# A recurrent-attention and wave-mixing kernel: r loaded by whole batches, w spread by a matmul, and tasks that may choose their engine

## The chip, the core and the metric

The kernel runs on one core of one Trainium2 chip. The metric is the device time of one execution in microseconds. Before the change the median of three runs is 149.64 us (148.95 to 150.03).

The engines are named as in the profile: PE multiplies matrices and writes to PSUM (eight banks here), DVE, ACT and POOL work on vectors, SP issues most DMAs. Only PE, DVE and ACT reach PSUM.

## What is computed

Inputs r, k, v have the shape (4 batches, 8 heads, 768 tokens, 48), w and u (8, 48). Cut to what matters:

```
state = 0
for t in range(768):                       # for every batch and head
    cur = outer(u * k[t], v[t])
    y[t] = r[t] @ (state + cur)
    state = w[:, None] * state + outer(k[t], v[t])
x = y, heads side by side                   # (4, 768, 384)

theta = x @ w_theta
zr, zi = x * cos(theta), x * sin(theta)
mixed = w_tok_r @ zr + w_tok_i @ zi         # over the 768 tokens of a batch
un = x + mixed
out = un + relu(un @ w_ch)
```

## The kernel before

**Chunks.** A batch has six chunks of 128 tokens, treated in three pairs. Within a chunk the recurrence becomes matmuls: r is multiplied by a power of w that grows with the token's place in its chunk (`wpow`), k by the inverse power (`wpinv`). Then scores k·r, masked to earlier tokens, take the place of the recurrence inside a chunk, and a state per chunk (`Y`, `Z`, and `Sb` in bf16) carries what came before.

**One pair of chunks (`front`, from L421).** Tokens lie on the 128 partitions.

- Load r, k and v of two chunks (`load_tokens`, L352): two DMAs each of 192 KB, one per chunk. A run of 48 floats, 192 bytes, lies together in DRAM for each head and token.
- L436 multiplies r by `wpow` into `Rw` (on POOL, one of the first pair on DVE); L448 multiplies k by `wpinv` into `Kw` (DVE); L456 casts v (ACT).
- `flip6` (L410) transposes eight blocks of `Rw` on PE (L414), and ACT evacuates them into `RT` (L417); the same for `Kw` into `KT`.
- Scores (L470, PE), masked products into `mAT` (L475, DVE); the diagonal with u: PD = RT·KT (L481, DVE), a small matmul (L489), its copy (L494, ACT), and `yd` (L496, POOL).
- Outer products for the state (L509, PE), `Y` (L521 and L523, DVE), `Z` (L526, POOL), `Sb` (L529, ACT).
- y from the carried state (L544) and the scores (L558), added into x (L564, DVE).
- x is transposed (`flip6` again), theta (L581, PE), its sine and cosine (L585, L588, ACT), then zr (L591, DVE) and zi (L594, POOL).

**Token weights (L391 to L405).** Twelve loads of 384 KB, rows of w_tok_r and w_tok_i, are transposed in fp32 on PE (L393) and evacuated, one half on ACT (L404), the other on DVE (L402).

**Mixing (`mixing`, from L599).** For each of six output chunks of a batch, three tasks of four matmuls (L613), the residual (L621, DVE), a transpose, the channel matmul (L629), and relu and residual (L634, DVE), and a store (L637).

**Setup (`setup`, from L274).** L275 loads w, repeated for all 128 partitions, into `w_f` (192 KB); ACT takes its logarithm (L328) and two exponentials (L332 `wpow`, L335 `wpinv`). u and w are also loaded in a small tile `wu` through ACT's queue (L283, L284) and transposed on PE (L315). Two loads of ACT's function tables stand at L326 and L340.

**The order.** No engine's order is written by hand. Every step is a task of a `Plan`: an engine, a planned cost in ns, what it reads and writes, the PSUM banks that it takes, and a due number (`prio`, smaller first). `order` (L83) plays the tasks through in planned time: each engine takes, of the tasks that are ready, the one with the lowest due number. PE is charged 95 ns for a change of tile form. POOL's tasks and DVE's marked ones exclude each other. `search` (L153) shifts random due numbers 2000 times and keeps a shift if the planned end does not grow. The instructions are then issued in that order. Loads have due numbers far below the rest and so keep the order in which the program creates them; 12 buffers (`Ls`) serve as a ring for all loads of r, k, v and weights. SP takes the loads in order, and a load waits there until its buffer has been read.

Of the kernel before, what the change touches and what calls it, by code (L numbers as in the profile page):

```python
# [17 lines left out]
BF16 = mybir.dt.bfloat16  # L18
Alu = mybir.AluOpType
Act = mybir.ActivationFunctionType  # L20

ROUNDS = 2000
# [8 lines left out]
PE, DVE, ACT, POOL, SP = "PE", "DVE", "ACT", "POOL", "SP"  # L31


KEEP = 0
SWITCH = 95.0
STAY = 10.0
LATENCY = {PE: 200.0, DVE: 150.0, ACT: 175.0, POOL: 160.0, SP: 2200.0}


class Task:  # L40
    __slots__ = ("eng", "ns", "fn", "deps", "prio", "seq", "lat", "acq", "uses", "nwait",
                 "users", "ready", "end", "mode", "keep", "port")


class Plan:

# [8 lines left out]
    def add(self, eng, ns, fn, rd=(), wr=(), prio=0.0, lat=None, acq=(), use=(), mode=0, keep=0, port=False):  # L55
        t = Task()
        t.eng, t.ns, t.fn, t.prio, t.mode = eng, ns, fn, prio, mode
        t.keep, t.port = keep, port or eng == POOL
        t.lat = LATENCY[eng] if lat is None else lat
# [19 lines left out]
        t.deps = deps  # L79
        self.tasks.append(t)  # L80
        return t

    def order(self):  # L83
        for t in self.tasks:
            t.users, t.nwait, t.ready = [], len(t.deps), 0.0
        for t in self.tasks:
            for d in t.deps:
                d.users.append(t)
        waiting = {e: [] for e in (PE, DVE, ACT, POOL, SP)}
        for t in self.tasks:  # L90
            if t.nwait == 0:
                waiting[t.eng].append(t)
        free_at = {e: 0.0 for e in waiting}
# [6 lines left out]
        while len(out) < n:  # L100
            for e in waiting:
                while free_at[e] <= now:
                    nfree = sum(1 for b in banks if b[0] <= now)
                    best = None
                    for t in waiting[e]:
                        if t.port and e in (DVE, POOL) and held[POOL if e == DVE else DVE] > now:
                            continue
                        if t.ready <= now and (
                                not t.acq or len(t.acq) + t.keep <= nfree):
                            rank = (t.prio - (STAY if e == PE and t.mode == last_mode and last_mode else 0.0), t.seq)  # L110
                            if best is None or rank < top:
                                best, top = t, rank
                    if best is None:
                        break
                    t = best
                    waiting[e].remove(t)
                    banks.sort()
                    for b in t.acq:
                        self.bank_of[b] = banks.pop(0)[1]
                    ns = t.ns  # L120
# [4 lines left out]
                    free_at[e] = now + ns  # L125
                    if t.port:
                        held[e] = now + ns
                    done = now + ns
                    t.end = done + t.lat
# [6 lines left out]
                    for x in t.users:  # L136
                        x.ready = max(x.ready, done if x.eng == e else t.end)
                        x.nwait -= 1
                        if x.nwait == 0:
                            waiting[x.eng].append(x)  # L140
            nxt = [f for f in free_at.values() if f > now]
            nxt += [t.ready for e in waiting for t in waiting[e] if t.ready > now]
# [10 lines left out]
    def search(self, rounds, seed=0):  # L153

        rnd = random.Random(seed)
        pool = [t for t in self.tasks if t.eng != SP]
        best = self.span()
        for _ in range(rounds):
            some = rnd.sample(pool, rnd.choice((1, 3, 10, 40)))
            old = [t.prio for t in some]  # L160
            scale = rnd.choice((2, 6, 20))
            for t in some:
                t.prio += rnd.gauss(0, scale)
            got = self.span()
            if got <= best:
                best = got
            else:
                for t, p in zip(some, old):
                    t.prio = p
        return best  # L170


def rows_of(w, n):
    return dataclasses.replace(w, ap=[[0, n]] + [list(x) for x in w.ap])


def wide(ap, n):
    return dataclasses.replace(ap, ap=[list(x) for x in ap.ap] + [[0, n]])
# [3 lines left out]
def kernel(  # L182
# [27 lines left out]
    bank_t = [ps.tile([C, 512], F32, name=f"bank{i}") for i in range(8)]  # L210

# [12 lines left out]
    mask01 = sb.tile([C, C], BF16, name="mask01")  # L224
    pi2 = sb.tile([C, 1], F32, name="pi2")
    wu = sb.tile([2 * HP, 2, Dp], F32, name="wu")
    w_f = sb.tile([C, H, D], F32, name="w_f")
    lw_f = sb.tile([C, H, D], F32, name="lw_f")
    lw_p = sb.tile([C, HP], F32, name="lw_p")
    tok_f = sb.tile([C, 2], F32, name="tok_f")  # L230
    wpow = sb.tile([C, H, D], F32, name="wpow")
# [5 lines left out]
    NL = 12  # L237
    Ls = ring(NL, [C, 2 * HD], F32, "ld")
    Rws = ring(2, [C, 2, H, Dp], BF16, "Rw")
    Kws = ring(4, [C, 2, H, Dp], BF16, "Kw")  # L240
    vbs = ring(5, [C, 2, H, D], BF16, "vb")
    RTs = ring(4, [C, 2, HP, C], BF16, "RT")
# [21 lines left out]
    def act_ns(n, psum=True):  # L264
        return n / 1.2 + (60 if psum else 95)

    def dve_ns(n, rate=1.0):
        return n / (0.96 * rate) + 75

    def pool_ns(n):  # L270
        return 190 + 1.95 * n


    def setup():  # L274
        P.add(SP, 300, lambda: nc.sync.dma_start(out=w_f, in_=rows_of(w, C)),  # L275
              wr=["w_f"], prio=-2e6, lat=3000)

        def wu_fill():
            nc.vector.memset(wu, 0.5)
        P.add(DVE, 100, wu_fill, wr=["wu"], prio=-100)  # L280

        def wu_load():
            nc.scalar.dma_start(out=wu[:HP, :, :D], in_=w.rearrange("(a b) d -> a b d", b=2))  # L283
            nc.scalar.dma_start(out=wu[HP:, :, :D], in_=u.rearrange("(a b) d -> a b d", b=2))  # L284
        P.add(ACT, 200, wu_load, wr=["wu"], prio=-99, lat=3000)

        def tok():
            nc.gpsimd.iota(tok_f[:, 0:1], pattern=[[0, 1]], base=0, channel_multiplier=1,
                           allow_small_or_imprecise_dtypes=True)
        P.add(POOL, 200, tok, wr=["tok_i"], prio=-100)  # L290

        def tok2():
            nc.vector.tensor_scalar(tok_f[:, 1:2], tok_f[:, 0:1], -1.0, -1.0,
                                    op0=Alu.mult, op1=Alu.add)
            nc.vector.memset(pi2, math.pi / 2.0)
            nc.vector.memset(uw, 0.0)
        P.add(DVE, 300, tok2, rd=["tok_i"], wr=["tok_f", "uw", "pi2"], prio=-99)
# [4 lines left out]
        P.add(POOL, 500, lambda: make_identity(nc, ident_f), wr=["ident_f"], prio=-98)  # L302
        P.add(POOL, 500, lambda: make_identity(nc, ident), wr=["ident"], prio=-98)
        P.add(POOL, 600, lambda: pads(Rws), wr=[(("Rw", i), j) for i in range(2) for j in range(2)], prio=-97)
        P.add(POOL, 800, lambda: pads(Kws), wr=[("Kw", i) for i in range(4)], prio=-96)

        def mask():
# [4 lines left out]
        P.add(POOL, 1000, mask, wr=["mask"], prio=-95)  # L312

        def wu_flip():
# [3 lines left out]
        P.add(PE, 300, wu_flip, rd=["wu", "ident_f"], acq=["wu"], prio=-90)  # L318
        P.add(DVE, 100, lambda: nc.vector.tensor_copy(wup, bank("wu")[:, :2 * HP]),
              use=["wu"], wr=["wup"], prio=-90)  # L320
        def uw_fill():
            for hi in range(2):
                q = slice(hi * Dp, (hi + 1) * Dp)
                nc.vector.tensor_mul(uw[q, :, hi], wup[q, HP:], wup[q, :HP])
        P.add(DVE, 200, uw_fill, rd=["wup"], wr=["uw"], prio=-90)
        P.add(ACT, 1300, lambda: nc.scalar.preload_act_table_set("natural_log_exp_and_others"),  # L326
              wr=["act_ln"], prio=-98.5)
# [357 lines left out]
```

## Time and profile before

| | |
|---|---|
| median of three runs | 149.64 us |
| profiled execution | 148.95 us |
| its span, first to last instruction | 147.2 us |
| outside the span | 1.75 us |
| PE busy | 130.2 us, 89% |
| DVE, ACT, POOL busy | 114.8, 92.0, 79.4 us |
| DMA packets | 81084, of these under 512 bytes 75561 |
| DMA queue of SP | 24.98 MB, 69.9% of 16 engines' span |
| first r half landed, second | 5.23, 6.08 us |
| last token weights landed | about 37.1 us |
| first score matmul, first mixing matmul | 11.41, 40.50 us |

"Busy" is the union of the times of an engine's instructions. A PE matmul's time includes its way through the array, and the next one starts before it ends; the rate is read from start to start. A wait is put down to what was released last. "x" with a number counts instructions.

### The profile page before, as it was taken

Reading aid. Unit: us, or ns where it says so; the run is one execution under the profiler, and the core shown is the slowest. Engines: PE = TensorE matmul, PEld = TensorE weight load, DVE = VectorE, ACT = ScalarE, POOL = GpSimd, SP = SyncE. Lnnn points to the kernel's source line nnn. Section 1 sums busy time; section 2 is a strip of 40 time slices with the busy share of each in tenths; the row PEclk is TensorE's granted clock in tenths of the full one; section 3 lists DMA queues with packets and bytes.
Section 4 is the critical chain, followed back from the end, with each engine's and each line's share of the span. In section 5 each row is a group of like instructions: output and inputs, shape, how many; then the busy total and the mean of one; then the engine's idle time right before and its main releaser. Section 6 shows DMA issues by size and latency. Waiting matters only on the chain.

```text
span 147.2 us, 4185 instructions
## 1 busy us (share of the span) xinstructions
PE 130.2 (89%) x1641; PEld 91.3 (62%) x1641; DVE 114.8 (78%) x220; ACT 92.0 (63%) x175; POOL 79.4 (54%) x96
## 2 busy tenths in 40 slices
PE   0157687999999999999989999999999999999990
PEld 0036574879966776667746666677666666656640
DVE  0349869699954989999979999999899998442561
ACT  3484667878949368689473984899735467702140
POOL 7317937473735649868469779691552747400000
PEclk9999999999999999999999999999999999999999
DMA  2999988999999799899998997995000111120224
GB/s 71 225 216 223 255 188 299 296 393 403 224 178 196 172 192 222 182 220 237 181 235 160 203 219 176 229 224 184 4 0 0 58 53 58 53 107 0 73 92 160
DMA packets 81084, 25.24 MB, mean 172 GB/s; under 512 B 75561, under 2 KB 79529, under 8 KB 81065
## 3 DMA queue, kind: packets, MB, share of 16 engines
q1 hardware_dynamic: 81040, 24.98, 69.9%
q8 instruction: 13, 0.21, 0.6%
q14 instruction: 7, 0.05, 0.1%
q10 hardware_dynamic: 24, 0.00, 0.0%
HBM read 20.25 MB, written 4.72 MB: 170 GB/s over the span
## 4 chain that ended last, share of the span: by engine, by line
PE 74%; DVE 7%; ACT 7%; DMA 6%; issue 3%; SPq 1%; DVEq 0%; ACTq 0%
PE bank_64 L613 8%; PE bank_65 L613 7%; PE bank_68 L613 4%; DMA ld_87<-in_v_dram 3%; DMA ld_86<-in_r_dram 3%; PE bank_63 L613 3%; PE bank_62 L613 3%; PE bank_68 L414 2%; PE bank_63 L414 2%; PE bank_63 L581 2%; PE bank_67 L613 2%; PE bank_61 L629 2%; PE bank_66 L414 2%; PE bank_64 L581 1%; PE bank_66 L613 1%
## 5 line engine op out<-in xcount | busy, mean ns | idle before, releaser
L613 PEld LDWEIGHTS <-WrT 128*128 128x128 bf16 x144 | 14.0, 97 | 7.8
L613 PEld LDWEIGHTS <-WiT 128*128 128x128 bf16 x144 | 14.1, 98 | 7.2
L526 POOL TENSOR_TENSOR Z_122<-Y_120,wC 128x192 f32<-128x192 f32 x12 | 7.8, 649 | 7.2 <-DVE Y_120 L521 4.0
L613 PE MATMUL bank_64<-zr_135,WrT 128*128 128x384 bf16 x30 | 9.8, 326 | 0.0
L613 PE MATMUL bank_64<-zi_137,WiT 128*128 128x384 bf16 x30 | 9.8, 326 | 0.0
L526 POOL TENSOR_TENSOR Z_123<-Y_121,wC 128x192 f32<-128x192 f32 x8 | 4.9, 617 | 7.3 <-DVE Y_121 L523 7.3
L613 PE MATMUL bank_65<-zr_135,WrT 128*128 128x384 bf16 x24 | 7.8, 327 | 0.0
L613 PE MATMUL bank_65<-zi_137,WiT 128*128 128x384 bf16 x24 | 7.8, 326 | 0.0
L436 POOL TENSOR_TENSOR Rw_95<-ld_88,wpow 128x384 bf16<-128x384 f32 x4 | 4.8, 1208 | 4.2 <-PE bank_67 L414 4.2
L436 POOL TENSOR_TENSOR Rw_96<-ld_85,wpow 128x384 bf16<-128x384 f32 x6 | 5.9, 1004 | 0.7 <-DMA ld_85<-in_r_dram 0.7
L594 POOL TENSOR_TENSOR zi_137<-x_132,sin_139 128x384 bf16<-128x384 bf16 x4 | 3.7, 932 | 4.3 <-ACT sin_139 L585 4.3
L613 PE MATMUL bank_62<-zi_138,WiT 128*128 128x384 bf16 x18 | 5.9, 326 | 0.0
L613 PE MATMUL bank_62<-zr_136,WrT 128*128 128x384 bf16 x18 | 5.9, 326 | 0.0
L594 POOL TENSOR_TENSOR zi_137<-x_134,sin_139 128x384 bf16<-128x384 bf16 x4 | 3.8, 964 | 3.6 <-ACT sin_139 L585 3.6
L315 PE MATMUL bank_61<-ident_f,wu 8*128 8x8 f32 x1 | 0.2, 239 | 5.7 <-DMA wu<-in_u_dram 5.7
L581 PEld LDWEIGHTS <-xT_142 128*128 128x128 bf16 x36 | 3.3, 98 | 2.6 <-ACT xT_142 L417 0.8
L594 POOL TENSOR_TENSOR zi_138<-x_132,sin_140 128x384 bf16<-128x384 bf16 x4 | 3.6, 913 | 2.4 <-ACT sin_140 L585 2.3
L414 PEld LDWEIGHTS <-Rw_95 128*128 128x128 bf16 x48 | 3.6, 111 | 2.0 <-POOL Rw_95 L436 1.4
L581 PEld LDWEIGHTS <-xT_141 128*128 128x128 bf16 x36 | 3.5, 103 | 2.1 <-issue 0.3
L436 POOL TENSOR_TENSOR Rw_96<-ld_91,wpow 128x384 bf16<-128x384 f32 x4 | 4.0, 998 | 1.5 <-DMA ld_91<-in_r_dram 0.8
L470 PEld LDWEIGHTS <-KT_110 64*128 64x128 bf16 x96 | 3.1, 101 | 2.7 <-ACT KT_110 L417 2.0
L436 POOL TENSOR_TENSOR Rw_95<-ld_94,wpow 128x384 bf16<-128x384 f32 x4 | 4.3, 1071 | 0.8 <-DVE Kw_98 L448 0.8
(593 smaller groups left out, 505.1 us busy)
## 6 DMA issues: line engine op xcount, KB each, us to landing
out_dram<-fin_150 SPq DMA_DIRECT2D x8, 192.0 KB, 2.0
out_dram<-fin_149 SPq DMA_DIRECT2D x8, 192.0 KB, 3.1
out_dram<-fin_151 SPq DMA_DIRECT2D x8, 192.0 KB, 2.0
ld_85<-in_r_dram SPq DMA_DIRECT2D x6, 192.0 KB, 4.6
ld_86<-in_k_dram SPq DMA_DIRECT2D x6, 192.0 KB, 3.6
ld_87<-in_v_dram SPq DMA_DIRECT2D x6, 192.0 KB, 4.0
ld_88<-in_r_dram SPq DMA_DIRECT2D x4, 192.0 KB, 4.1
ld_89<-in_k_dram SPq DMA_DIRECT2D x4, 192.0 KB, 3.6
```

Source lines behind the costliest of these rows:

```text
L315: nc.tensor.matmul(bank("wu")[:, :2 * HP], wu.rearrange("p a d -> p (a d)"), ident_f[:2 * HP, :2 * HP], is_transpose=True, start=True, sto ...
L414: nc.tensor.matmul(bank16(tok)[:, i * C:(i + 1) * C], s, ident, is_transpose=True, start=(i == 0), stop=(i == n - 1))
L436: lambda c=c, vec=vec, Rw=Rw, ir=ir: vec.tensor_mul(Rw[:, c, :, :D], Ls[ir][:, c * HD:(c + 1) * HD].rearrange("p (h d) -> p h d", h=H), wpow),
L470: nc.tensor.matmul(bank(tk[hi])[:, hp * C:(hp + 1) * C], KT[q, c, hp, :], RT[q, c, hp, :], start=(hp == 0), stop=(hp == HP - 1))
L526: P.add(POOL, pool_ns(HP * D) - 70, lambda cc=cc: nc.gpsimd.tensor_mul(Zs[cc % 2], Ys[cc % 2], wide(wC, D)), rd=[("Y", cc % 2), "wC"], wr= ...
L581: nc.tensor.matmul(bank(th)[:, :HD], xT[:, t, dk, :], Wth[:, dk, :], start=(dk == 0), stop=(dk == ND - 1))
L594: P.add(POOL, pool_ns(HD), lambda sn=sn, to=to, t=t: nc.gpsimd.tensor_mul(zi[:, to], x[:, to], sn[:, t]), rd=xk + [("sin", g % 2, t)], wr= ...
L613: nc.tensor.matmul(bank(tm)[:, :HD], WT[:, so, to * C:(to + 1) * C], z[:, so], start=(so == 0 and i == 0), stop=(so == NCH - 1 and i == 1))
L629: nc.tensor.matmul(bank(tf)[:, :HD], uT[:, dk, :], Wch[:, dk, :], start=(dk == 0), stop=(dk == ND - 1))
```

## The change

Three things are done at once.

**r of a whole batch.** In place of one load for each pair, `load_batch` makes two DMAs for each batch, each of four heads and all 768 tokens (590 KB). Partition p gets the tokens 6p to 6p+5, so that 288 floats, 1152 bytes, lie together. The tile `Lr` has one buffer and is not part of the ring, which shrinks to ten. A partition now holds six tokens (n = 0 to 5) with different places in their chunk, so there are six tiles of powers of w (`wpow[:, n]`, scale (6p+n) mod 128). Six products make `Rw` of the whole batch (one buffer); for each of four head pairs six blocks are transposed into one bank, and the evacuation puts the tokens in order, reading PSUM with a step of 128 elements. `RT` holds a batch (two buffers). Scores, PD and the carried product read it there.

**w.** A load of 1.5 KB puts w on one partition; a matmul with a row of ones (K = 1) spreads it over 128 partitions in PSUM. Logarithm and exponentials read PSUM. The second table load gets the due number 3 in place of -93.

**Tasks and search.** A task names one or more engines with a cost for each; the search changes due numbers and, for tasks with several, the engine. A task whose turn it is may now wait for the port that DVE and POOL share, or let another go first. Costs and latencies are new numbers. A mixing task takes a bank only with four others free, as long as its batch's zr and zi are not all issued; the carried product is made to wait for the masked scores. 1500 rounds replace 2000.

The core of the diff (the forms of the tasks that only gain engines are the same for the rest):

```
-ROUNDS = 2000
+LATENCY = {PE: 200.0, DVE: 130.0, ACT: 190.0, POOL: 130.0, SP: 2300.0}
+SLACK = 150.0
+ROUNDS = 1500
...
     def search(self, rounds, seed=0):
+        multi = [t for t in pool if len(t.ways) > 1]
...
+            turn = rnd.sample(multi, rnd.choice((0, 0, 1, 2))) if multi else []
+            old = [(t, t.prio, t.eng) for t in some + turn]
...
+            for t in turn:
+                t.eng = rnd.choice([e for e in t.ways if e != t.eng])
...
-    w_f = sb.tile([C, H, D], F32, name="w_f")
-    wpow = sb.tile([C, H, D], F32, name="wpow")
+    w_1 = sb.tile([1, HD], F32, name="w_1")
+    wpow = sb.tile([C, NCH, H, D], F32, name="wpow")
...
-    NL = 12
+    NL = 10
-    Rws = ring(2, [C, 2, H, Dp], BF16, "Rw")
+    Lr = sb.tile([C, H, NCH, D], F32, name="Lr")
+    Rw = sb.tile([C, NCH, H, Dp], BF16, name="Rw")
-    RTs = ring(4, [C, 2, HP, C], BF16, "RT")
+    RTs = ring(2, [C, HP, S], BF16, "RT")
...
+    def two_inputs(n):
+        return [pool(n), dve(n, 1.0, True)]
+    def from_psum16(n):
+        return [act(n), dve(n, 2.0)]
...
+        P.add([(PE, 660)], lambda e: nc.tensor.matmul(bank("lw")[:, :HD], ones, w_1, start=True,
+                                                      stop=True),
+              rd=["ones", "w_1"], acq=["lw"], prio=-92)
+        for n in range(NCH):
+            P.add([(ACT, 390)], lambda e, n=n: nc.scalar.activation(
+                wpow[:, n].rearrange("p h d -> p (h d)"), bank("lw")[:, :HD], Act.Exp,
+                scale=tok_f[:, 2 + n:3 + n]),
+                rd=["tok_f", "act_ln"], use=["lw"], wr=[("wpow", n)], prio=-96.5 + 0.1 * n)
...
+    def load_batch(b, src):
+        for hf in range(2):
+            _, pri = slot(False)
+            hs = slice(hf * HP, (hf + 1) * HP)
+            P.add([(SP, 1550)], lambda e, hs=hs: nc.sync.dma_start(
+                out=Lr[:, hs].rearrange("p h n d -> p h (n d)"),
+                in_=src[b, hs].rearrange("h (p n) d -> p h (n d)", n=NCH)),
+                wr=[("Lr", hf)], prio=pri)
...
+        load_batch(b, r)
+        for n in range(NCH):
+            ways = two_inputs(HD)
+            P.add(ways if b else ways[::-1], lambda e, n=n: vec[e].tensor_mul(
+                Rw[:, n, :, :D], Lr[:, :, n, :], wpow[:, n]),
+                rd=[("Lr", 0), ("Lr", 1), ("wpow", n)], wr=[("Rw", n)], prio=base)
+        for hp in range(HP):
+            flip_blocks(RT[:, hp].rearrange("p (q n) -> p q n", n=NCH),
+                        [Rw[:, n, 2 * hp:2 * hp + 2, :] for n in range(NCH)],
+                        ("TR", b, hp), base, [("Rw", n) for n in range(NCH)], [rT[hp]],
+                        "p (n q) -> p q n")
```

Tasks that get a choice: the r and k products and yd and Z (POOL or DVE), PD (DVE or POOL), the evacuations of transposes (ACT or DVE), the token weights' evacuations (ACT or DVE), the casts of v, of the square weights and of the state (ACT, DVE or POOL), zi (POOL or DVE), the copy of the diagonal and the first `Y` (ACT or DVE).

## The prediction

> **What bounds the kernel now.** I read the windows first, then the waits of PE, then the timelines of PE, ACT and the DMA queue where PE is not full.
>
> Busy time by stage (start:end, length, then PE, weight loads, DVE, ACT, POOL, granted clock, DMA share, GB/s):
>
> ```profile
> 0.00:10.00 10.00, 2.35 (x17) 1.56 (x17) 3.15 (x10) 5.20 (x8) 4.17 (x18) 1.00 0.81 164
> 10.00:20.00 10.00, 6.20 (x106) 5.28 (x108) 6.94 (x13) 6.64 (x11) 7.45 (x8) 1.00 1.07 228
> 28.00:40.00 12.00, 12.00 (x152) 10.33 (x152) 10.86 (x22) 9.69 (x23) 6.18 (x7) 1.00 1.01 334
> 60.00:80.00 20.00, 19.31 (x259) 13.02 (x257) 18.34 (x35) 13.25 (x25) 14.14 (x16) 1.00 0.97 209
> 100.00:120.00 20.00, 20.00 (x295) 13.50 (x293) 19.13 (x39) 12.53 (x26) 8.39 (x11) 1.00 0.10 34
> ```
>
> From 28 us on PE is full; DMA is nearly full up to 100 us and idle afterwards, without PE noticing. So PE's own work is the bound after 28 us, and only the head is slack. PE's longest waits, all but two of them in the head:
>
> ```profile
> PE bank_64 L470 <- ACT KT_110 L417: 1.7, 1, 1.7
> PE bank_61 L414 <- DVE x_132 L564: 1.3, 1, 1.3
> PE bank_62 L414 <- POOL Rw_95 L436: 1.3, 1, 1.3
> PE bank_65 L544 <- ACT Sb_124 L529: 0.9, 1, 0.9
> PE bank_61 L581 <- ACT xT_142 L417: 0.7, 1, 0.7
> ```
>
> A second loss hides inside "busy". The same 128-column score matmuls, early and later (start, length):
>
> ```profile
> 11.49 0.31 PE L470 MATMUL bank_64<-RT_106,KT_110 64*128 64x128 bf16 x1
> 11.60 0.31 PE L470 MATMUL bank_64<-RT_106,KT_110 64*128 64x128 bf16 x1
> ...
> 29.58 0.22 PE L470 MATMUL bank_65<-RT_108,KT_110 64*128 64x128 bf16 x1
> 29.64 0.22 PE L470 MATMUL bank_65<-RT_108,KT_110 64*128 64x128 bf16 x1
> ```
>
> They follow each other by 0.11 us early and by 0.055 us later, although the granted clock reads 1.00 in every row. The slow rate lasts to about 28.3 us (weight transposes fall from 0.85 us for three at 27.56 to 0.57 at 28.68); PE's last gap of the head ended at 23.26. So full speed came 5.0 us after PE became continuous.
>
> **The loss in one number.** By 28.3 us PE had done 54 transposes (0.056 us each at full speed), 32 score matmuls (four groups of 0.30), 6 of theta (0.163 each), 6 weight transposes (0.109 each) and small ones (2.6): 3.0 + 1.2 + 1.0 + 0.65 + 2.6 = 8.5 us. So 28.3 - 8.5 = 19.8 us are lost at the head. From 28.3 to 142.1 it works without a pause but for 0.9 us (0.7 at 75, 0.2 at 87), so its work is 8.5 + 113.8 - 0.9 = 121.4 (113.8 = 142.1 - 28.3). The tail from 142.1 is 5.1. Check: 19.8 + 121.4 + 0.9 + 5.1 = 147.2, the span. The change leaves the number of transposes and matmuls as it is (96 transposes of r in 12 groups of 8 become 96 in 16 of 6), plus one matmul in the head. So it can move only the 19.8, the 0.9 and the order's own overhead.
>
> **The change, part by part.**
>
> *w by a matmul, six powers of w instead of one.* The ACT rows of before (start, length):
>
> ```profile
> 4.39 0.52 ACT L328 ACTIVATE lw_f<-w_f 128x384 f32<-128x384 f32 x1 [2.31 <-DMA w_f<-in_w_dram]
> 4.95 0.61 ACT L335 ACTIVATE wpinv<-lw_f,tok_f 128x384 f32<-128x384 f32 x1
> 5.47 0.60 ACT L332 ACTIVATE wpow<-lw_f,tok_f 128x384 f32<-128x384 f32 x1
> 8.13 1.28 ACT L340 ACT_TABLE_LOAD   x1
> 9.42 1.02 ACT L417 ACTIVATE RT_106<-bank_62 128x1024 bf16<-128x1024 bf16 x1
> ```
>
> The 192 KB w_f landed 3.6 us after its issue. The 1.5 KB load takes its place: between 3.0 (from the ends of the u load's issue at 3.00 to its use at 5.65 are 2.65, plus 0.35 of issue) and 3.6, so landed at 3.8 to 4.4; I take 4.0. The K=1 matmul has no row: at the least three fp32 transposes at the early rate, 3 x 0.21 = 0.64, at the most twice that; I take 0.7, nearest to the transposes. Then Ln 0.52 and six Exp at 0.52 from start to start, 3.1: the last wpow at about 8.6, wpinv at 9.1. Before, both stood at 6.07. The second table load moves behind this (its due number goes from -93 to 3), so the 1.28 at 8.13, which held RT_106 from 8.24 to 9.42, leaves the path.
>
> *r whole.* Two loads of 590 KB go ahead of k and v on SP's queue. Weight loads (1536-byte runs) land 1.0 us apart for 393 KB; pairs of token loads (192-byte runs) about 1.75. Between the two by bytes and runs a 1152-byte run makes 1.18 MB in some 3.1 us, against 5.2 for three pairs; bounds 3.0 and 5.2. r lands near 7, under the Exp chain (cover: wpow, 8.6; if r took 5.2 it would land near 9 and cost 0.4). k0 and v0 behind it come 1.3 us later than before, all later loads of batch 0 some 2 earlier. The queue also loses its stop between 21.03 and 23.72, where a weight load waited for a ring slot. The last token weights, landed at 37.1 before, should land at 31 to 33. Every later batch saves 2.1 us of DMA; that is hidden (PE full), except the 0.9, which begins with a late v:
>
> ```profile
> 69.07 4.70 DMA ld_87<-in_v_dram
> 73.89 0.29 issue
> 74.20 0.40 issue
> 74.60 0.80 ACT xT_142 L417
> 75.45 0.66 PE bank_61 L581 x3
> ```
>
> I take the 0.9 as gone. A load that waits on SP now also waits for Lr (one buffer): the next r load stands until the batch's six products are done, early in the batch, and outputs behind it wait no longer than now.
>
> *First scores.* Six products of 0.55 on DVE follow the Exps (the last at 9.2), then 24 transposes at 0.107 = 2.6, K's 8 = 0.86 and KT's evacuation 1.02: first scores at 14.0, against 11.41. That is 2.6 later. The four RT evacuations (768 columns; xT's 0.80 is the same size) go beside it on ACT and DVE.
>
> *What comes back.* Pairs 1 and 2 no longer need an r load, r products (POOL 1.0 each), 8 transposes and 1.02 of ACT each; only k is between them and their scores. Before, gaps of 1.29, 0.56, 0.53 and 0.90 lay between 13 and 23.3. Now K1 and K2's transposes, scores 1 and the outer products are at hand as soon as pair 0 runs: about 3.7 us of full-speed work, 7.4 at half rate, for the 5.5 us from 14 to 19.5, and the first token weights land at about 20 instead of 24.3. So PE is close to continuous from about 18, and at full speed by 22 to 24. By 23 it has done 1.8 (r and K0) + 2.8 (14 to 19.5 at half rate) + 2.2 (to 23, part fast) = 6.8: loss 16.2, against 19.8. Gain 3.6.
>
> *Tasks on several engines.* No work is taken away by it. In 28 to 40 us DVE is 10.9 of 12 busy and POOL 6.2, so some K products, PD (0.69 on DVE) and casts can leave DVE; in 80 to 100 DVE is 19.6 of 20 with PE at 19.75, so what PE gains at the head must be fed there. Gain 0 taken; bounds: the order's overhead in 28.3 to 142.1 is about 4 us (113.8 less the 0.9, against 110 if every matmul kept the median spacing of its line), so +2 or -2.
>
> *RT's evacuation reads PSUM with a step* of 128 elements. No row does that. Lower bound 0.80 as xT; upper twice that, 1.6, since no row shows more than a doubling between forms of one size. L564 writes with a stride at 0.55, as L621 does without, so I take 0.80. Upper end: +1.6 at the head (two in a row on each of two engines), 13 us more on ACT in all, which has 55 idle.
>
> The Trainium skill, Advanced Engine Details and Errata, PSUM Cachelines, says that every two neighbouring elements should be contiguous for best throughput; it speaks of a penalty and gives no size for ACT. It speaks against this change; by it the sum would be up to 1.6 higher. No row here shows it.
>
> The Trainium skill, TensorE: Matmul & The Clock Gate, What's actually happening, has PE at half rate until about 3.4 us of sustained work. The 5.0 us above agree in kind, but no row of the granted clock does. By its 3.4 the sum would be about 0.8 lower.
>
> **Sum.** Loss 16.2 + work 121.4 + no gap + tail 5.1 = 142.7 of span; with the 1.75 around the span (148.95 - 147.2) 144.45. The profiled execution is the fastest of three, 0.7 under the median of 149.64; in terms of the median 145.1, and I say 145.0.
>
> **The rivals.**
>
> *B, nothing comes back* (13%): the head's start is 2.6 later and the pairs recover just that. PE is full from 28 anyway, DMA was hidden. Only the 0.9 goes: 148.7, range 147.9 to 151. For it: 12.00 of 12 at 28 to 40. Against it: the first 20 us hold 8.5 busy of 20.
>
> *C, DVE becomes the bound of batch 0, slower* (17%). Before, DVE's last zr of batch 0 starts at 39.55, and the first mixing matmul at 40.50; DVE is busy 10.9 of 12 before it. The change gives DVE up to five more r products of 0.55 (2.7) and starts the scores 2.6 later. If the search leaves them and the K products there, the last zr comes 5 later, mixing starts near 45.5, and the weight transposes that fill PE until 40.3 are over sooner: span +4, 153.5. It decides once the last zr of batch 0 starts after 40. Against it: POOL is idle half of that time and the tasks may go there.
>
> *D, the head falls away more fully* (20%): PE continuous from 15 and fast from 19 to 20, loss 12 to 13, overhead 1 to 2 lower: 139.5 to 141.5. For it: r stands ready for all pairs and weights land 5 us sooner. Against it: DVE, as in C.
>
> **How the numbers follow.** The forecast (50%) is 145.0, by itself 141.5 to 147.9 (loss 14 to 19, overhead +-1). A measurement here tells about 1% from no change, 148.1 to 151.1. Faster: forecast 50 + D 20 + a little of B 2 = 72%. Same: 11%. Slower: 17%. For 8 in 10 the range runs from 139.5 (D's end) to 151.5: it leaves out most of C and a few beyond D.
>
> **What would show it.** wpow's last Exp ending near 8.6; r landing near 7; first L470-like scores near 14; PE's spacing falling to 0.055 by 22 to 24, not 28; the last token weights landed by 33; mixing from 36 to 37, not 40.5; no wait of PE on xT near 75. Wrong if first scores come after 16, if the r evacuations take 1.6, if the last zr of batch 0 starts after 40, or if PE shows new waits on DVE or POOL after 28: an order made from planned costs that the chip does not keep.

## The result and the profile after

The changed kernel takes 159.19 us (median, 157.45 to 160.68) against 149.64: 1.061 times the time before, with a 95% interval of 1.050 to 1.071. The ratio leaves out the slowest of the four executions (160.68), which the chip ran in a slower state. The forecast was 145.0. The profiled execution has 157.45 us and a span of 155.7, 8.5 more than the 147.2 of before.

The windows of after, same columns as those of before (start:end, length, PE, weight loads, DVE, ACT, POOL, granted clock, DMA share, GB/s):

```profile
0.00:10.00 10.00, 1.86 (x3) 0.67 (x3) 3.48 (x15) 6.20 (x12) 3.44 (x17) 1.00 0.94 199
10.00:20.00 10.00, 6.89 (x112) 6.46 (x112) 5.99 (x12) 8.18 (x12) 3.02 (x2) 0.88 1.34 219
28.00:40.00 12.00, 12.00 (x177) 9.71 (x175) 11.45 (x25) 10.54 (x25) 5.12 (x6) 1.00 1.03 312
60.00:80.00 20.00, 17.20 (x250) 11.81 (x249) 17.43 (x34) 14.17 (x29) 15.63 (x17) 1.00 1.11 215
100.00:120.00 20.00, 19.29 (x242) 12.92 (x241) 20.00 (x38) 9.01 (x20) 7.92 (x8) 1.00 0.13 47
```

The row to look at is 60 to 80: PE had 19.31 of 20 before and has 17.20 now. The forecast moved only the head; what moved is the middle. PE's waits:

```profile
PE bank_63 L481 <- DVE Rw L497: 3.5, 1, 3.5
...
PE bank_62 L535 <- ACT RT_105 L318: 1.5, 1, 1.5
PE bank_66 L481 <- ACT dg_123 L318: 1.4, 1, 1.4
PE bank_61 L608 <- ACT KT_107 L318: 1.4, 1, 1.4
PE bank_61 L465 <- DMA ld_93<-in_moe_w_tok_r_dram: 1.2, 1, 1.2
PE bank_63 L553 <- DVE mAT_111 L540: 1.0, 1, 1.0
PE bank_61 L481 <- DVE zr_133 L656: 1.0, 1, 1.0
```

Before, all but two of the long waits were in the head. To see where the time is lost, I take from the time elapsed the full-speed duration of all matmuls done by then (120.7 us in the whole kernel, before and after):

| loss of PE, us, up to | 30 | 50 | 70 | 90 | 120 | 140 | end |
|---|---|---|---|---|---|---|---|
| before | 19.9 | 20.1 | 20.5 | 22.2 | 22.5 | 22.2 | 26.5 |
| after | 20.1 | 21.4 | 25.5 | 29.1 | 30.6 | 30.7 | 35.0 |
| k, v in long runs | 18.8 | 20.2 | 22.2 | 24.0 | 25.7 | 25.7 | 30.0 |
| loads planned as measured | 20.6 | 21.3 | 25.0 | 27.3 | 28.2 | 28.1 | 32.5 |
| w alone | 18.8 | 19.6 | 21.0 | 23.4 | 24.6 | 24.7 | 28.9 |
| w and r | 21.2 | 21.3 | 23.7 | 25.1 | 26.1 | 26.0 | 30.2 |

(The last four rows are experiments told below.) The head of after costs the same as before, and of the 8.5 us that the span grew by, 6.7 are lost between 30 and 90 us, while the DMA queue is full (9.0 against 2.3), and 1.6 from 90 to 140.

One such loss, on DVE (start, length, and in brackets the idle time before it with what ended it):

```profile
48.95 0.90 DVE L513 TENSOR_TENSOR Kw_97<-ld_91,wpinv 128x384 bf16<-128x384 f32 x1 [0.69 <-DMA ld_91<-in_k_dram]
...
52.98 0.56 DVE L513 TENSOR_TENSOR Kw_98<-ld_93,wpinv 128x384 bf16<-128x384 f32 x1 [0.95 <-DMA ld_93<-in_k_dram]
53.46 0.99 DVE L546 TENSOR_TENSOR PD_110<-RT_106,KT_108 128x1024 bf16<-128x1024 bf16 x1
54.38 0.68 DVE L540 TENSOR_TENSOR mAT_111<-bank_63,mask_71 128x512 bf16<-128x512 f32 x1
```

what PD_110 and the masks needed, on ACT and PE:

```profile
51.87 0.83 ACT L318 ACTIVATE RT_106<-bank_66 128x768 bf16<-128x768 bf16 x1
52.98 0.23 PE L535 MATMUL bank_63<-RT_106,KT_108 64*128 64x128 bf16 x1
```

and the chain of waits through it:

```profile
47.50 0.99 SPq L421
48.54 4.35 DMA ld_93<-in_k_dram
52.98 0.56 DVE Kw_98 L513
53.54 0.91 DVE PD_110 L546
54.45 1.20 DVE mAT_111 L540 x2
```

Kw_98 is the k product of the *next* batch (batch 2, pair 0). The order puts it on DVE ahead of PD and two masks of batch 1. Its load lands at 52.9; the order, made at build, had planned 46.4. The last input of PD, RT_106, was written at 52.70, and PD starts at 53.46, behind Kw_98; the masks, whose scores began at 52.98, stand behind PD, and PE behind the masks (the 1.0 at L553). So this one late load holds DVE up by at most 0.8 us. ACT stands in the same way at its casts of v:

```profile
ACT vb_102 L318 <- DMA ld_86<-in_v_dram: 2.4, 1, 2.4
...
ACT vb_101 L318 <- DMA ld_84<-in_v_dram: 1.9, 1, 1.9
```

The kernel's own plan gives each load a landing time. Against it (planned, then landed, us): first token weights 19.0, about 23.2; second r half of batch 1 34.3, 39.3; of batch 2 49.5, 57.3; of batch 3 70.6, 82.3; a v load of batch 3 75.2, 87.8. The lateness grows from 4 to 12.6 us while the queue is full. In before it went from 0 (18.2, 18.2) to 5 (94.5, 99.5). The change had lowered the planned cost of a 192 KB token load from 1050 to 890 ns. The chain shows what SP needs to issue one, from the first microseconds on (start, length):

```profile
7.63 1.00 SPq L421
...
8.68 0.98 SPq L421
...
9.70 0.97 SPq L421
```

They land at the same pace, early (8.03, 9.08, 10.14 us) and late (67.77, 68.84, 69.89, 70.95). In before, token loads that follow each other land faster, early (8.73, 9.44, 10.41) and late (56.39, 57.29, 58.20, 59.07, 59.84): some 0.9 apart. So the changed kernel's own token loads are slower than before's. That goes with the new w: here is SP's queue (packets, MB, share of 16 engines' span) in the kernel with w alone (run 9 below) and in before:

```profile
q1 hardware_dynamic: 80898, 24.78, 75.5%
```

```profile
q1 hardware_dynamic: 81040, 24.98, 69.9%
```

Share times span is 112.9 us (of 149.6) against 102.9 (of 147.2), for slightly fewer bytes. All six kernels with the new w and r by pairs have 110.8 to 116.0 us here, and the other three with the old w (runs 6, 13 and 14) 102.5 to 102.6. Why is open. One thing that goes with it: the ring's tiles start at a multiple of 64 bytes of a partition in the kernels with the old w, and 32 bytes past one in all others (a new tile of 24 bytes, `tok_i`, stands ahead of them). No run varies this alone, so it is not shown to be the cause.

Yet all loads of after are done by 88 us, those of before by 101. They are not late against before, only against the order. In the page's row of the chain's shares this is SP's queue, which before had 1%:

```profile
PE 60%; DVE 12%; SPq 11%; DMA 7%; ACT 4%; issue 3%; DVEq 0%; ACTq 0%
```

### The profile page after: what moved, and what is told of

It reads as the page before. It is cut to its first block, busy times and chain, and to the rows that moved or that the text cites. A ratio compares the mean times of both kernels' runs of the same rounds, so it can differ in the third digit from the quotient of the medians.

```text
span 155.7 us, 4142 instructions
## 1 busy us (share of the span) xinstructions
PE 132.7 (85%) x1643; PEld 92.0 (59%) x1643; DVE 121.0 (78%) x242; ACT 87.5 (56%) x172; POOL 72.5 (47%) x89
## 2 busy tenths in 40 slices
DMA packets 60205, 25.05 MB, mean 161 GB/s; under 512 B 50713, under 2 KB 58650, under 8 KB 60186
## 3 DMA queue, kind: packets, MB, share of 16 engines
q1 hardware_dynamic: 60162, 24.78, 66.7%
## 4 chain that ended last, share of the span: by engine, by line
PE 60%; DVE 12%; SPq 11%; DMA 7%; ACT 4%; issue 3%; DVEq 0%; ACTq 0%
SPq L421 9%; PE bank_63 L678 6%; PE bank_61 L678 6%; PE bank_64 L678 5%; PE bank_62 L678 4%; DMA ld_93<-in_moe_w_tok_r_dram 4%; DMA ld_93<-in_k_dram 3%; PE bank_68 L678 3%; PE bank_66 L678 2%; SPq L440 2%; PE bank_66 L646 1%; PE bank_67 L646 1%; DVE mAT_112 L540 1%; DVE zr_132 L656 1%; DVE mAT_111 L540 1%
## 5 line engine op out<-in xcount | busy, mean ns | idle before, releaser
L497 POOL TENSOR_TENSOR Rw<-Lr,wpow 128x384 bf16<-128x384 f32 x18 | 19.6, 1106 | 10.2 <-PE bank_65 L623 3.7
L591 POOL TENSOR_TENSOR Z_119<-Y_117,wC 128x192 f32<-128x192 f32 x12 | 7.2, 602 | 6.6 <-DVE Y_117 L320 2.8
L481 PEld LDWEIGHTS <-Rw 128*128 128x128 bf16 x96 | 6.8, 111 | 3.9 <-DVE Rw L497 3.6
L591 POOL TENSOR_TENSOR Z_120<-Y_118,wC 128x192 f32<-128x192 f32 x8 | 4.1, 508 | 7.1 <-DVE Y_118 L587 7.1
L481 PE MATMUL bank_63<-ident,Rw 128*128 128x128 bf16 x24 | 2.3, 242 | 3.5 <-DVE Rw L497 3.5
L535 PEld LDWEIGHTS <-KT_107 64*128 64x128 bf16 x96 | 2.9, 94 | 3.7 <-issue 2.8
L646 PEld LDWEIGHTS <-xT_139 128*128 128x128 bf16 x36 | 3.3, 97 | 2.7 <-ACT xT_139 L318 0.6
L513 POOL TENSOR_TENSOR Kw_97<-ld_89,wpinv 128x384 bf16<-128x384 f32 x1 | 1.0, 994 | 8.1 <-DMA ld_89<-in_k_dram 8.1
L535 PEld LDWEIGHTS <-KT_108 64*128 64x128 bf16 x96 | 3.1, 101 | 2.7 <-issue 1.9
L646 PEld LDWEIGHTS <-xT_138 128*128 128x128 bf16 x36 | 3.4, 97 | 2.2 <-issue 0.4
L318 ACT ACTIVATE uT_143<-bank_67 128x384 bf16<-128x384 bf16 x2 | 1.0, 490 | 6.5 <-issue 4.6
L546 DVE TENSOR_TENSOR PD_109<-RT_105,KT_107 128x1024 bf16<-128x1024 bf16 x4 | 2.7, 682 | 2.4 <-ACT RT_105 L318 2.4
```

What stands on the lines that cost most here:

```text
L318: nc.scalar.activation(dst, src, Act.Copy)
L481: nc.tensor.matmul(bank16(tok)[:, i * C:(i + 1) * C], s, ident, is_transpose=True, start=(i == 0), stop=(i == n - 1))
L497: P.add(ways if b else ways[::-1], lambda e, n=n: vec[e].tensor_mul(Rw[:, n, :, :D], Lr[:, :, n, :], wpow[:, n]), rd=[("Lr", 0), ("Lr", 1) ...
L535: nc.tensor.matmul(bank(tk[hi])[:, hp * C:(hp + 1) * C], KT[q, c, hp, :], RT[q, hp, cc * C:(cc + 1) * C], start=(hp == 0), stop=(hp == HP ...
L546: vec[e].tensor_mul(PD, RT[:, :, 2 * pr * C:2 * (pr + 1) * C].rearrange("p h (a t) -> p a h t", a=2), KT), rd=[kT] + rT, wr=[kP], prio=pb + 4)
L591: P.add(two_inputs(HP * D), lambda e, cc=cc: vec[e].tensor_mul(Zs[cc % 2], Ys[cc % 2], wide(wC, D)), rd=[("Y", cc % 2), "wC"], wr=[("Z", c ...
```

## The experiments

Theory **L**: the order runs ahead of the loads, because they are planned too short. Rivals: **W**, the whole-batch r with its single buffer makes a chain at each batch's start; **S**, the random search only drew a bad order; **K**, the reserve of four banks for mixing; later **H** (the head behind the K=1 matmul), **R** (the order's new rules), **M** (the choice of engines costs on the chip). The "planned end" is the kernel's own number from its planner, not a measurement; with it goes the distance from there to the end of the span. Ratios are against before, measured beside each run (medians 148.75 to 149.93 us), with 95% intervals.

**1. Same order, faster loads.** k and v are read in runs of 1536 bytes. A partition then gets other tokens, so y is not the reference's; order and sizes stay.

```
-                in_=src[b, :, t0:t0 + C, :].transpose([1, 0, 2])),
+                in_=src[b].rearrange("h t d -> (h t d)").rearrange("(p f) -> p f", p=C)[:, (2*pr+c)*HD:(2*pr+c+1)*HD]...
```

> Three theories stand. L (late loads): the order fixed at build plans a 192 KB token load at 0.89 us and half of r at 1.55 us; the loads come later and later against that plan (the last ones land 12.5 us after the planned time, those of the kernel before only 3.5), and engines that work in order stand behind them. W (whole r): at the start of a batch the load, six products, 24 transposes and four evacuations must all end before the first scores, and PE has nothing else. S (search): the order found is a poor draw. This kernel keeps the changed kernel's order and instructions; only k and v are read from DRAM in runs of 1536 bytes instead of 192 (so tokens get other tokens' k and v; the same bytes are moved). L expects the distance of span and planned end (12.5 us) to fall to that of the kernel before (5.8): span 149, time 150 to 151. W expects 155 to 157, since the chain from r to the scores is not touched but for an earlier landing. S expects 157 to 159, as the changed kernel.

Measured: 152.74 us, 1.021 [1.014, 1.027]. Four of the six per cent go without any change of order. The page's packets show the edit (60205 before it), and PE has 19.49 in 60 to 80, where it had 17.20:

```profile
DMA packets 17198, 25.05 MB, mean 166 GB/s; under 512 B 1562, under 2 KB 15643, under 8 KB 17179
```

```profile
60.00:80.00 20.00, 19.49 (x285) 13.02 (x284) 19.34 (x38) 16.72 (x34) 16.34 (x19) 1.00 0.77 255
```

It fits L, came slower than L said (150 to 151), and leaves 2% open. (The 3.5 that the expectation gives for before is 5.0 by the landing above, 94.5 and 99.5.)

**2. r by pairs again,** the rest of the change as it is (`Rws`, four `RT`, one `wpow`, `NL = 12` as before).

> Undoes one part alone: r is loaded by pairs of chunks again (192-byte runs, twelve ring buffers, one tile of powers of w, eight transposes per pair), while the w matmul, the tasks on several engines, the new costs and the search stay. Its planned end is 142.9 us, the changed kernel's 143.2. W expects most of the loss to vanish: 149 to 151.5. L expects little: token loads are still planned at 0.89 us and there are more of them, 155 to 160. S expects 152 to 159, a new draw.

Measured: 163.89 us, 1.093 [1.086, 1.099]; span 162.1 with a planned end of 142.9. W falls: the kernel becomes slower, since r in short runs fills the queue further (115.1 us of queue time against 103.9). L had the sign; the size is over its range.

**3. No bank reserve** (`keep=4` to `keep=0`).

> The changed kernel, in which a mixing task no longer has to leave four PSUM banks free (the number 4 becomes 0, as before the change). Planned end 141.1 in place of 143.2. If the reserve starved PE of mixing work (a fourth theory, K), the time falls to 150 to 152; L and W expect only the planned 2 us, 155 to 157; S expects anything from 152 to 159.

Measured: 159.33 us, 1.063 [1.055, 1.070], span 158.2, planned end 141.1. K falls. L's 155 to 157 fails too: a lower planned end was worth nothing, as the order lay even further ahead of the loads.

**4. Loads planned as they are.**

```
-            P.add([(SP, 890)], lambda e, c=c, t0=t0: nc.sync.dma_start(
+            P.add([(SP, 1050)], lambda e, c=c, t0=t0: nc.sync.dma_start(
-            P.add([(SP, 1550)], lambda e, hs=hs: nc.sync.dma_start(
+            P.add([(SP, 2100)], lambda e, hs=hs: nc.sync.dma_start(
```

> The changed kernel with two planned costs raised to what the trace shows: a token load 1.05 us (as the kernel before has it), half of r 2.1 us. Planned end 146.9. L expects the distance between span and plan to fall from 12.5 to about 6: span 152.5 to 153, time 154 to 155. W expects no gain, 156 to 159, since the work between r and the scores stays. S expects 155 to 160.

Measured: 154.85 us, 1.032 [1.025, 1.039]. The planned end is 3.7 *later* (146.9 after 143.2), the span 2.5 shorter: the distance falls from 12.5 to 6.3, near before's 5.8. SP's queue is gone from the chain:

```profile
PE 65%; DVE 22%; DMA 3%; ACT 3%; issue 3%; POOL 0%; ACTq 0%; DVEq 0%
```

**5. The same two edits with r by pairs** (1050; there is no r half).

> The pair version of r (as in the run with pairs) with token loads planned at 1.05 us again. Planned end 144.8. L, as it stands after the first four runs (span = plan + about 6 when loads keep their plan; plan + 12 to 19 when they do not), expects span 151, time 152 to 153.5, eleven below the same kernel with loads planned at 0.89. What is left of W (a batch-wide r delays the first scores of batches 1 to 3, some 3 us) expects it 2 to 4 below the batch-wide version with real load costs (154.85): 151 to 153. S expects 153 to 164.

Measured: 154.36 us, 1.035 [1.028, 1.042], above the ranges of L (152 to 153.5) and of W (151 to 153). One number is worth some 5.8% here (1.093 without it). W falls again: pairs and whole batches (1.032) are equal within the intervals once loads are planned as measured.

**6. The kernel before, with the load cost of after.** The test from the other side:

```
-            P.add(SP, 1050, lambda c=c, t0=t0: nc.sync.dma_start(
+            P.add(SP, 890, lambda c=c, t0=t0: nc.sync.dma_start(
```

> The kernel before with one number changed: a token load planned at 0.89 us as in the change, in place of 1.05. Planned end 140.1 in place of 141.4. L expects the order to run ahead of the loads as in the pair version: span 154 to 159, time 156 to 161. W and S, which see nothing wrong in the planned cost, expect 148 to 151.

Measured: 154.55 us, 1.036 [1.026, 1.046], slower by more than its planned end (140.1, 1.3 earlier) would let one hope. L holds in sign and is smaller than it said. The lateness of the loads grows as in after, to 12.4 us (a v load planned at 83.7 lands at 96.1), though this kernel's token loads keep the faster pace: on average, with outputs and stops between them, 0.89 is too short here too. The profile shows the same picture as after, ACT standing at v (before: 1.5 the longest):

```profile
ACT vb L456 <- DMA ld<-in_v_dram: 11.3, 10, 2.6
```

**7. Two buffers for r,** with loads planned as measured (`Lrs = ring(2, ...)`, `Lrs[b % 2]`).

> The changed kernel with real load costs (1.05 and 2.1 us) and a second buffer for r of a batch, so that the load of the next batch's r no longer stands until the products of this one have ended. Planned end 145.2 in place of 146.9. If the single buffer is what is left of W: span about 151.3, time 152.5 to 153.5. If not: 154 to 156.

Measured: 153.05 us, 1.028 [1.021, 1.035]; the time lies in the range given for a cost of the single buffer, but against 1.032 with one buffer the intervals overlap, and the planned end is 1.7 us earlier. The single buffer is not shown to cost anything.

**8. Another draw** of the changed kernel's search (`seed=1`).

> The changed kernel with another seed of the search (planned end 143.4, against 143.2). S expects a scatter of several us, 152 to 164. L expects the same lateness of the loads and so 156 to 160.

Measured: 157.05 us, 1.051 [1.042, 1.060]. The draw is worth about 1%, not 6: S explains a part at most, as far as two draws tell.

Some 3% remained with true loads. The next four put the old rules of the order back (no reserve, the carried product not waiting for masks, old latencies, no waiting for the port, due number -93 for the table load, 300 ns for an output, 2000 rounds), plan the loads as measured, and add the parts one by one: `multi = []` takes the choice away, r by pairs takes the whole batch away. The planned costs of all other tasks stay the change's, so "w alone" is before with the new w and these costs.

**9. w alone.**

> Only w is spread by the K=1 matmul; r is loaded by pairs, one engine for each task, and the rules and latencies of the order are those of before (a load is planned at 1.05 us, no bank reserve, no wait of the carried product for the masks). Its own planned end is 142.9 us, that of before 141.4. Theory L (the loads planned too short made the order; nothing else is wrong on the chip): a plan with true loads is kept with the 5.8 to 7.8 us of distance seen so far, so span 148.7 to 150.7 and time 150.5 to 152.5. Rival R (the rest of the gap is in the order's new rules): the same time as before within 1%, 148 to 150. Rival H (the K=1 matmul and the head behind it cost the rest): 152 to 155, and the first scores come later than in before (11.4 us).

Measured: 153.01 us, 1.019 [1.014, 1.025], span 149.6; above L's range and inside H's. But H's reason falls: its first scores start at 10.1, 1.3 earlier than before, and its loss at 30 us is 1.1 lower. The time is lost between 50 and 120 us. SP's queue is 8% of its chain, where before had 1%: with the slower token loads, a plan of 1.05 us each does not free the chain of the queue.

**10. w and the choice of engines.**

> As the run with w alone, and tasks may choose their engine. Planned end 142.8 us. L: as w alone within 1 us, 150.5 to 152.5. Rival M (the choice of engines itself costs on the chip, because work put on POOL or DVE runs against the port that they share and the plan misses it): 2 us or more above w alone, up to the 154.4 of the pairs with real loads.

Measured: 154.66 us, 1.031 [1.026, 1.035], 1.65 above w alone at nearly the same planned end (142.8, 142.9). Between the two theories; M's 2 us are not reached.

**11. w and r.**

> r of a whole batch in one buffer and w by the matmul, one engine for each task, the old rules, loads planned as they were measured. Planned end 143.7 us, 0.9 above w alone. L: 151.2 to 153.2. Rival W (the chain at the start of a batch is the cost, whatever the plan says): 3 us or more above w alone. First scores near 16 us either way, as r's two halves land at 5.3 and 7.0 and 24 transposes follow.

Measured: 153.49 us, 1.024 [1.019, 1.029]. L's 151.2 to 153.2 just missed, W's three above w alone far off. First scores at 17.5:

```profile
17.51 0.29 PE L536 MATMUL bank<-RT,KT 64*128 64x128 bf16 x4
```

The loss at 30 us is 2.4 above w alone, 1.3 at the end: r whole is paid in the head and given back in part, as far as one draw of each tells.

**12. All three, old rules.**

> All three parts of the change, loads planned as measured, the order's old rules (no reserve, no wait for the masks, old latencies, a task does not wait for the port). Planned end 144.1 us; the kernel with real loads and the new rules had 146.9 and took 154.9 us. L with R: the 2.8 us of the plan come back on the chip, 151.5 to 153.0. L without R: 154 to 156, as the rules are only the planner's. Whatever the rules, a time at or below that of before would say that nothing but planning was wrong.

Measured: 155.08 us, 1.032 [1.027, 1.037], as with the new rules (1.032). R falls: 2.8 us in the plan, nothing on the chip. SP's queue, gone from the chain in run 4, has 9% of it here.

The next runs ask how much of these small differences is the draw.

**13. Before, seed 2.**

> The kernel before with seed 2 in its search, nothing else. Planned end 142.0 us against 141.4 of the kernel before. Theory S2 (the parts cost little, the kernel before is a lucky draw): 151 to 153, like the parts. Theory P (the parts cost what the plan says, the draw moves less than 1%): 149.5 to 151.

**14. Before, seed 4.**

> The kernel before with seed 4. Planned end 141.2 us, the lowest of five seeds. S2: 150.5 to 153. P: 148.5 to 150.5.

Measured: 0.998 [0.994, 1.003] and 1.008 [1.004, 1.012] (medians 150.03 and 150.75 against 149.93), the slower one with the *lower* planned end. Before is no lucky draw by more than about 1%.

**15. w alone, seed 4.**

> Only w by the matmul, old rules, one engine for each task, seed 4. Planned end 141.9 us, against 142.9 with seed 0, which took 153.0. P: a lower plan carries over, 150.5 to 152. S2: anything from 149 to 153.5, without regard to the plan.

Measured: 150.25 us, 1.003 [0.999, 1.007]. Two draws of w alone lie 1.6% apart, so its 1.9% of run 9 is not told apart from the draw.

**16. All three, old rules, seed 2.**

> All three parts with loads planned as measured and the old rules, seed 2. Planned end 143.6 us, against 144.1 with seed 0, which took 155.1. P: 153.5 to 155. S2: 151 to 156.

Measured: 155.75 us, 1.041 [1.034, 1.048], again slower with the lower planned end.

**17. w and the choice, seed 4.**

> w by the matmul and tasks with a choice of engine, r by pairs, old rules, loads planned as measured, seed 4. Planned end 141.9 us, the same as w alone with seed 4, which was 0.3% above before. M (the choice costs on the chip what the plan does not see): 1% or more above that run, so 152 us or later. Rival S2 (only the draw): within 1% of it, 149.5 to 151.5.

Measured: 152.65 us, 1.020 [1.015, 1.025], 1.7% above run 15 with the same seed and planned end (141.9). That is M's range. But the same seed is not the same draw: with a choice the search uses up other random numbers.

**18. w and r, seed 1.**

> w by the matmul and r of a whole batch in one buffer, one engine for each task, old rules, loads planned as measured, seed 1. Planned end 143.8 us, as with seed 0 (143.7), which was 2.4% above before. Theory P (r's later first scores cost what the plan says): 152.5 to 154.5. S2: 150 to 152.

Measured: 152.09 us, 1.019 [1.014, 1.024]; between the theories' ranges.

All draws together, as ratios to before:

| | draws | mean |
|---|---|---|
| before | 1.000, 0.998, 1.008 | 1.002 |
| w | 1.019, 1.003 | 1.011 |
| w, r | 1.024, 1.019 | 1.022 |
| w, choice, loads as measured | 1.035 (new rules), 1.031, 1.020 | 1.029 |
| w, r, choice, loads as measured | 1.032 (new rules), 1.032, 1.041 | 1.035 |
| the change: the same, loads short | 1.061, 1.051 | 1.056 |

By the means the change is 5.4 points above before. Of these 2.1 are the short load costs, 1.3 to 1.7 the choice, 0.6 to 1.0 r by whole batches and 0.9 w. Draws of one version lie up to 1.6 apart. The short load costs stand clear of that: with them before is at 1.036, the change at 1.061 and 1.051, the change with pairs at 1.093, each above all draws of the same version without them (and with faster loads, run 1, the change's own order is at 1.021). The choice raised the time in each pair that differs by it alone (runs 9 and 10, 15 and 17, 11 and 12: 1.1, 1.7, 0.7 points), which makes a cost likely and not certain. r and w are not told apart from the draw. No version of the change beats the kernel before.

Why the choice would cost is not shown. The distance from the planned end to the span's end is 5.8 to 8.1 us in six kernels with loads planned at 1.05 us or more and one engine for each task (before, runs 9, 11, 13, 14, 18), mean 6.6; with the choice 6.0 to 10.5 in seven (runs 4, 5, 7, 10, 12, 16, 17), mean 8.2. The ranges overlap. PD moved to POOL kept its planned 2.17 us (2.11 to 2.13, but for one of 2.64 in run 2). Some other moves were planned too short: r's stepped evacuation on DVE 0.48 us, taken 0.94 to 0.96; a v cast on DVE 0.48, mostly taken 0.55, once 0.85. There are one to three of each in a kernel that has them, and which of them decides was not tried.

## Why the prediction was wrong, point by point

- **What failed first: "PE is full from 28 on, DMA is hidden".** Everything after 28.3 us was carried over from before (work 121.4, no gap), with the order's overhead put at 0, +-2. It held for the order of before, whose loads stay within 5 us of the plan. The change makes a new order from new costs, and I noted "costs and latencies are new numbers" without pricing one. Measured: 8.3 us more lost after 30 than before; load costs planned as measured take 4.3 us off the time (159.2 to 154.9, 1.061 to 1.032). The term behind it is the token load: I carried 1.75 us for a pair over, 0.88 each, which agrees with the new 890 and with before, early and late. In after the same load takes about 1.05 (rows 7.63 to 9.70 and the landings above). Before's trace could not show that. What it could show is that loads planned at 1.05 still fell 5 us behind, which leaves no room for a lower number.
- **"All later loads of batch 0 some 2 earlier", queue freed, last token weights at 31 to 33:** the last landed at 34.6 (before 37.1), the first at 23.2 (before 24.3, forecast 20). Right in direction, half in size or less: the twelve loads of k and v that come ahead of them cost some 0.15 us more each, together about 2 us (an estimate from the landings above).
- **"PE close to continuous from about 18, full speed by 22 to 24":** wrong, 23.31 and about 28, as before (23.26 and 28.3). The gain of 3.6 did not come; the loss at 30 is 20.1 against 19.9. The head went rival B's way, mixing starting at 40.08 (before 40.50).
- **First scores 14.0:** 16.31. The K=1 matmul took 1.61 us in two pieces against 0.7 (upper end 1.28), but w landed at 2.2 and not 4.0, so the logarithm started at 3.88, ahead of the forecast. Then the order made ACT and DVE stand at the small load of u and w, which let PE start on it only at 7.05 (its use in before: 5.65): ACT idled 1.15 us, because the logarithm `lw_p` stands in the middle of the exponentials, and the six products of r ran from 7.88 to 10.78, where the forecast had them done at 9.2. The last wpow ended at 9.2 instead of 8.6. The table load at 9.26, ahead of the first RT evacuation, cost nothing there: ACT idled another 1.15 us behind it, waiting for PE.

```profile
7.53 0.20 ACT L389 ACTIVATE lw_p<-wup 128x4 f32<-128x4 f32 x1 [1.15 <-DVE wup L381]
...
8.20 1.04 ACT L392 ACTIVATE wpow<-bank_61,tok_f 128x384 f32<-128x384 f32 x2
9.26 1.28 ACT L401 ACT_TABLE_LOAD   x1
11.70 0.81 ACT L318 ACTIVATE RT_105<-bank_63 128x768 bf16<-128x768 bf16 x1 [1.15 <-PE bank_63 L481]
...
15.44 0.82 ACT L318 ACTIVATE RT_105<-bank_64 128x768 bf16<-128x768 bf16 x1
```

  All four evacuations went to ACT, one after the other, with KT between them, until 16.26; I had spread them over ACT and DVE.
- **r lands near 7:** right, its halves at 5.26 and 6.99.
- **RT's stepped read 0.80:** right on ACT, 0.81 to 0.82 in the rows above. The rule of the Trainium skill, Advanced Engine Details and Errata, PSUM Cachelines, shows no price on ACT here: xT, 768 columns without a step, takes 0.81 as well. On DVE it does: one such evacuation took 0.94, xT there 0.55. Runs 7, 8, 12 and 16 have it at 0.95 to 0.96.
- **Choice of engines 0, +-2:** 1.3 to 1.7 points by the means, 2 to 2.5 us, at the upper bound or above it, and not clear of the draw.
- **Rival C (DVE the bound of batch 0):** its sign came, the last zr of batch 0 starting at 44.87 (before 39.55), but not its mechanism: mixing started at 40.08 with the pairs that were ready, the two late zr (44.02, 44.87) waited for ACT with DVE idle before them (0.87 and 0.29), and by 50 us only 1.3 more was lost than before, against the 4 that C named. The loss of C's size came by the mechanism that only the last sentence named, an order made from planned costs that the chip does not keep. It should have been a rival with a price.
- **The 0.9 near 75 us** (a late v) did not go; waits of that kind multiplied.

## What to carry to other kernels

A static order is only as good as the costs it is made from: where loads were planned too short, in-order engines stood at the late load with ready work behind them. (No run planned a load too long, so what that costs is not shown.) Check planned costs against the trace of the changed kernel and not of the one before, since a change can alter the cost of a load that it does not touch, as here. Compare planned with real landing times; a planned end by itself ordered these kernels badly (runs 3, 4, 12, 14, 16). Where a search with random draws makes the order, one draw on each side does not tell a part worth 1%.

## What the runs showed of the chip

PE reached the full rate early in after and lost it again. The first scores follow each other on a bank by 0.055 us at 16.3; from 18 to 28 the rate is half (0.10 to 0.11 for the next scores, at 18.0), and here the granted clock shows it, which read 1.00 in the slow head of before:

```profile
14.00:16.00 2.00, 0.83 (x13) 0.74 (x11) 0.00 (x0) 2.00 (x3) 0.00 (x0) 1.00 1.12 273
16.00:18.00 2.00, 1.39 (x42) 1.20 (x43) 1.71 (x3) 2.00 (x4) 0.03 (x1) 0.90 1.32 215
18.00:20.00 2.00, 1.50 (x32) 1.35 (x32) 2.00 (x5) 1.84 (x4) 2.00 (x1) 0.50 1.37 230
...
26.00:28.00 2.00, 2.00 (x15) 2.00 (x14) 0.99 (x3) 1.22 (x3) 0.00 (x0) 0.54 1.03 410
28.00:30.00 2.00, 2.00 (x35) 1.37 (x33) 1.89 (x5) 1.37 (x4) 0.46 (x1) 1.00 1.01 364
```

PE stood for more than half of 14 to 16, 1.5 us in one piece up to 16.31; the full rate is back 4.5 us after it became continuous at 23.31 (before: 5.0). The Trainium skill, TensorE: Matmul & The Clock Gate, What's actually happening, gives about 3.4 us of sustained work, in windows that do not start with the work; both kernels needed more than one such window and less than two.

Run length moves the queue more than bytes: 17198 packets in place of 60205 for the same 25.05 MB brought SP's queue from 66.7% to 48.1% of the 16 engines' span (103.9 to 72.5 us, run 1).
